# A chunked RWKV-7 recurrence with a gated feed-forward on one Trainium2 core: small TensorE tiles, back substitution on VectorE and a hand-written PE order

## Chip, cores and metric

The kernel runs on one core of a Trainium2 chip. The metric is the device time of one execution in microseconds (us). The kernel before took 1751.07 us, the median of three runs between 1740.38 and 1788.12.

## What is computed

Inputs are r, k, v, w, a, b of shape (4, 8, 768, 40) (batch, heads, steps, head width) and two weight matrices. For each of the 32 (batch, head) pairs a 40x40 state goes through 768 steps; the outputs are the rows of a 3072x320 matrix, and a feed-forward block follows:

```python
for t in range(S):
    y[:, :, t] = np.einsum('bhd,bhde->bhe', rt, state)
    Sa = np.einsum('bhde,bhe->bhd', state, at)
    state_decay = state * wt[:, :, None, :] - np.einsum('bhd,bhe->bhde', Sa, bt)
    state = state_decay + np.einsum('bhd,bhe->bhde', vt, kt)
...
h = x @ w_in          # 320 -> 2048
g = h * np.cos(h)
return (g @ w_out).astype(np.float32)   # 2048 -> 320
```

All arithmetic is float32. The two weight matrices arrive as float64 and are put together as float32 on the chip.

## The kernel before

The 768 steps are cut into 24 chunks of 32. Four batches times 32 steps fill the 128 partitions; the eight heads lie in the free dimension, and in transposed operands as four pairs of heads of 64 rows each (40 used). Names and lines are those of the listing below.

`prep(c)` (L208) makes what does not depend on the state. It transposes w, a, k, b, v, r (`turned`, L199), runs the product of decays with a scan (L217), divides (L219), and forms the products `gram` (L237 to 260). The inverse of a triangular 32x32 matrix per (batch, head), I + N, comes from five doubling steps (L262 to 289): VectorE transposes 32x32 blocks (L265) into a block-diagonal 128x128 tile `pbd`, PE multiplies with it (`power`), ScalarE and VectorE copy and add. `ttbd` holds the inverse, also block-diagonal.

`chain(c, ...)` (L302) carries the state over the chunk: `x0ps` (right-hand side), `snps` (times the inverse), `upd` (new state, L327 to 346), `sTps` and `mps` (the same solution transposed, times r), `yps` (outputs), `strn` (the new state transposed, through a multiplication with the identity), and four transposes `xps` that bring the outputs into `xT` for the feed-forward.

`first` (L402) and `second` (L423) are the feed-forward. `first` multiplies 256 tokens (two chunks) with w_in (`ph`, and a 64-row rest `w_in_tail`, in two row halves), and forms h*cos(h) with three VectorE and two ScalarE passes; `second` multiplies with w_out (`po`).

A matmul is recorded at the helper's line, L84; groups are told apart by their tiles. PSUM holds two buffers for `prep`, two for `chain`, three for `ph`, one for `po`. The order on every engine is made by a scheduler from the program's order: chunk c's `chain`, loads of chunk c+2 on SP's queue, `prep(c+1)`, then a part of the feed-forward of the two chunks before (`later`). The weights are read on ScalarE's DMA queue after `prep(0)`, in 28 pieces, each going through four VectorE, four GpSimd and one ScalarE instruction (`rounded`, L139).

Of the kernel before, what the change touches and what calls it, by code (L numbers as in the profile page):

```python
# [10 lines left out]
I32 = mybir.dt.int32  # L11
# [9 lines left out]
def kernel(  # L21
# [63 lines left out]


    nat = {n: kept(f"nat_{n}", [P, H, DP], 2, 1.0 if n == "w" else 0.0) for n in "wkabvr"}
# [3 lines left out]
    def load(c):  # L91
        for n in "wkabvr":
            for i in range(B):
                nc.sync.dma_start(
                    nat[n][c % 2][blk[i], :, :D],
                    src[n][i, :, c * C : (c + 1) * C, :].rearrange("h t d -> t h d"),
                )

    load(0)
    kn_b = kept("kn", [P, H, DP], 2, 0.0)  # L100
    bn_b = kept("bn", [P, H, DP], 2, 0.0)
    w0 = kept("w0", [P, NQ * B, C], 1, 0.0)[0]
    w1 = kept("w1", [P, NQ * B, C], 1, 0.0)[0]
    wx = kept("wx", [P, NQ * B, C], 1, 1.0)[0]
    pbd = kept("pbd", [P, 2, NQ, P], 1, 0.0)[0]
    ttbd_b = kept("ttbd", [P, 2, NQ, P], 2, 0.0)
    x0 = kept("x0", [P, 2, NQ, DP], 1, 0.0)[0]
    vbd = kept("vbd", [P, B, H, D], 1, 0.0)[0]
    snbd = kept("snbd", [P, B, 2, NQ, D], 1, 0.0)[0]
    st_b = kept("st", [P, NQ, B, DP], 2, 0.0)  # L110
# [4 lines left out]
    su = kept("su", [P, P], 1, 1.0)[0]  # L115

    nc.gpsimd.affine_select(
        su, su, pattern=[[1, P]], compare_op=ALU.is_gt, fill=0.0, base=0, channel_multiplier=-1
    )
    for s, base in ((1, 0), (-1, C - 1)):  # L120
        nc.gpsimd.affine_select(
            su, su, pattern=[[-C * s, B], [0, C]], compare_op=ALU.is_ge, fill=0.0, base=base,
            channel_multiplier=s,
        )
    su_c = kept("su_c", [P, C])[0]
    ident_c = kept("ident_c", [P, C])[0]
    for i in range(B):
        nc.gpsimd.tensor_copy(su_c[blk[i], :], su[blk[i], blk[i]])
        nc.gpsimd.tensor_copy(ident_c[blk[i], :], ident[blk[i], blk[i]])
    half_pi = kept("half_pi", [P, 1], 1, math.pi / 2)[0]  # L130
    su_q = su.unsqueeze(1).to_broadcast([P, NQ, P])
# [7 lines left out]
    def rounded(dst, src, by):  # L139


        n, cols = dst.shape[0], dst.shape[-1]
        words = sb2.tile([P, 512, 2], I32, tag="words", name="words")[:n, :cols]
# [347 lines left out]
```

## Time and profile before

| what | value |
|---|---|
| median of three runs | 1751.07 us |
| the profiled execution: its time | 1756.64 us |
| its span, first to last instruction | 1754.9 us |
| mean granted TensorE clock, of full speed (2.4 GHz) | 0.791 |
| instructions | 33475 |
| moved over HBM | 34.08 MB read, 3.93 MB written |

The profile comes from one execution. PE is TensorE's matmul part, PEld its weight loads, DVE VectorE, ACT ScalarE, POOL GpSimd, SP the queue of the sync engine, which issues DMAs. Busy time is the union of an engine's instructions; a matmul's own duration holds the depth of the pipeline, so that the pace of a run of matmuls is read from where the next group starts, not from the mean duration. The granted clock is the share of 2.4 GHz that TensorE was given; it has two levels, 0.5 and 1.

### The profile page before, as it was taken

Reading aid. Unit: us, or ns where it says so; the run is one execution under the profiler, and the core shown is the slowest. Engines: PE = TensorE matmul, PEld = TensorE weight load, DVE = VectorE, ACT = ScalarE, POOL = GpSimd, SP = SyncE. Lnnn points to the kernel's source line nnn. Section 1 sums busy time; section 2 is a strip of 40 time slices with the busy share of each in tenths; the row PEclk is TensorE's granted clock in tenths of the full one; section 3 lists DMA queues with packets and bytes.
Section 4 is the critical chain, followed back from the end, with each engine's and each line's share of the span. In section 5 each row is a group of like instructions: output and inputs, shape, how many; then the busy total and the mean of one; then the engine's idle time right before and its main releaser. Section 6 shows DMA issues by size and latency. Waiting matters only on the chain.

```text
span 1754.9 us, 33475 instructions
## 1 busy us (share of the span) xinstructions
PE 1664.4 (95%) x14464; PEld 1394.4 (79%) x14464; DVE 858.3 (49%) x1575; ACT 364.6 (21%) x796; POOL 154.5 (9%) x269
## 2 busy tenths in 40 slices
PE   4686999999999999999999999999999999999998
PEld 3676887887878888788788788788787888888876
DVE  8767453444454355355445444445436437436423
ACT  1122222131121122122212213113113112113112
POOL 3556000000000000000000000000000000000000
PEclk8555888778667778987878888878878889779779
DMA  4333111001100111111111100110010011000000
GB/s 84 93 88 76 17 20 19 14 12 19 24 12 12 20 16 20 20 16 20 20 16 18 20 16 15 20 20 13 16 28 12 12 23 21 13 13 1 1 9 8
DMA packets 165523, 40.20 MB, mean 23 GB/s; under 512 B 158720, under 2 KB 161792, under 8 KB 165376
## 3 DMA queue, kind: packets, MB, share of 16 engines
q1 hardware_dynamic: 161280, 27.57, 9.9%
q10 hardware_dynamic: 4096, 10.49, 2.0%
q8 instruction: 115, 1.88, 0.5%
q14 instruction: 32, 0.26, 0.0%
HBM read 34.08 MB, written 3.93 MB: 22 GB/s over the span
## 4 chain that ended last, share of the span: by engine, by line
PE 85%; DVE 9%; ACT 2%; issue 1%; POOL 1%; DMA 1%; SPq 0%; ACTq 0%; DVEq 0%; POOLq 0%
PE ph L84 16%; PE power L84 15%; PE po L84 14%; PE yps L84 9%; PE gram L84 6%; PE strn L84 6%; PE turned L204 5%; PE x0ps L84 4%; PE snps L84 3%; DVE pbd L265 2%; PE upd L84 2%; PE mps L84 2%; DVE rw L219 2%; ACT snbd L322 1%; PE xps L396 1%
## 5 line engine op out<-in xcount | busy, mean ns | idle before, releaser
L84 PEld LDWEIGHTS power<-pc,pbd 128*128 128x128 f32 x1920 | 282.2, 232 | 67.8 <-issue 49.4
L84 PE MATMUL power<-pc,pbd 128*128 128x64 f32 (+1 forms) x1920 | 291.5, 314 | 32.2 <-DVE pbd L265 28.1
L84 PE MATMUL ph<-xT,w_in_sb 128*128 128x256 f32 x768 | 246.6, 462 | 1.7 <-DVE gT L421 1.2
L84 PE MATMUL po<-w_out_sb,gT 128*128 128x320 f32 x768 | 247.4, 476 | 0.5 <-ACT ot L430 0.5
L265 DVE STREAM_TRANSPOSE pbd<-pc 32x256 f32<-32x256 f32 x480 | 208.3, 434 | 80.7 <-ACT pc L279 71.8
L84 PEld LDWEIGHTS po<-w_out_sb,gT 128*128 128x128 f32 x768 | 155.2, 210 | 61.6 <-issue 16.8
L84 PEld LDWEIGHTS ph<-xT,w_in_sb 128*128 128x128 f32 x768 | 164.6, 232 | 35.5 <-issue 11.0
L279 ACT COPY pc<-power 128x256 f32<-128x256 f32 x96 | 35.7, 372 | 518.3 <-PE power L84 512.3
L84 PE MATMUL ph<-xT,w_in_tail 64*128 64x256 f32 x384 | 112.8, 447 | 0.0
L283 DVE TENSOR_TENSOR pc<-power,pc 128x256 f32<-128x256 f32 x72 | 30.6, 425 | 158.1 <-ACT pc L279 157.9
L84 PE MATMUL yps<-bn,mbd 128*128 128x40 f32 x384 | 103.3, 364 | 0.0
L84 PE MATMUL yps<-kn,rvbd 128*128 128x40 f32 x384 | 100.9, 357 | 2.2 <-DVE mbd L360 2.2
L84 PE MATMUL strn<-ident,st 64*64 64x40 f32 x1472 | 98.2, 307 | 0.0
L84 PEld LDWEIGHTS strn<-ident,st 64*64 64x64 f32 x1472 | 94.7, 217 | 2.3 <-DVE frac L151 0.2
L217 DVE TENSOR_TENSOR_SCAN wp<-w,w 128x512 f32<-128x512 f32 x24 | 30.0, 1251 | 131.9 <-ACT w L215 131.9
L220 POOL COPY wx<-wp 128x496 f32<-128x496 f32 x24 | 14.3, 597 | 868.4 <-DVE wp L217 823.4
L84 PEld LDWEIGHTS yps<-kn,rvbd 128*128 128x128 f32 x384 | 84.2, 271 | 6.4 <-DVE mbd L360 3.1
L84 PEld LDWEIGHTS yps<-bn,mbd 128*128 128x128 f32 x384 | 86.8, 278 | 0.0
L389 ACT COPY s_nat<-strn 128x320 f32<-128x320 f32 x46 | 19.6, 425 | 313.3 <-PE strn L84 313.3
L84 PEld LDWEIGHTS ph<-xT,w_in_tail 64*128 64x128 f32 x384 | 59.9, 207 | 30.2 <-issue 25.0
L376 DVE TENSOR_TENSOR x<-yps,wxn 128x160 f32<-128x160 f32 x48 | 15.6, 325 | 139.5 <-PE yps L84 139.5
L219 DVE RECIPROCAL rw<-wp 128x512 f32<-128x512 f32 x24 | 80.3, 3347 | 0.4
(116 smaller groups left out, 2179.8 us busy)
## 6 DMA issues: line engine op xcount, KB each, us to landing
words<-in_moe_w_out_dram ACTq DMA_DIRECT2D x16, 320.0 KB, 3.0
words<-in_moe_w_in_dram ACTq DMA_DIRECT2D x8, 512.0 KB, 3.9
nat_w<-in_w_dram SPq DMA_DIRECT2D x96, 40.0 KB, 2.1
nat_k<-in_k_dram SPq DMA_DIRECT2D x96, 40.0 KB, 2.2
nat_a<-in_a_dram SPq DMA_DIRECT2D x96, 40.0 KB, 2.1
nat_b<-in_b_dram SPq DMA_DIRECT2D x96, 40.0 KB, 2.3
nat_v<-in_v_dram SPq DMA_DIRECT2D x96, 40.0 KB, 2.1
nat_r<-in_r_dram SPq DMA_DIRECT2D x96, 40.0 KB, 2.1
```

Of the source, the lines that this page charges most:

```text
L84: nc.tensor.matmul(o, lhsT=lhsT, rhs=rhs, start=start, stop=stop, skip_group_check=True)
L204: nc.tensor.transpose(ps[:, q, :], x[:, q, :], ident)
L217: nc.vector.tensor_tensor_scan(flat(wp), flat(w0), flat(w1), 0.0, ALU.mult, ALU.add)
L219: nc.vector.reciprocal(seq(rw), wp)
L220: nc.gpsimd.tensor_copy(wx[:, :, 1:], wp[:, :, : C - 1])
L265: nc.vector.transpose(pbd[blk[i], :, :, blk[i]].rearrange("p e q t -> p (e q) t"), heads(pc)[blk[i], :, 0, :],)
L279: nc.scalar.copy(heads(new)[:, :, 0, :], ps[:, :, 0, :])
L283: nc.vector.tensor_tensor(heads(new)[:, :, 1, :], ps[:, :, 1, :], heads(pc)[:, :, 1, :], ALU.add)
L322: nc.scalar.copy(snbd[blk[i], i], ps[blk[i]])
L376: nc.vector.tensor_tensor(by_parity(x)[:, e], ps, by_parity(g["wxn"])[:, e], ALU.mult)
L389: nc.scalar.copy(new_s[:, q0 : q0 + 2], ps)
L396: nc.tensor.transpose(ps[: min(P, DM - d0), i, :], xf[:, d0 : min(d0 + P, DM)], ident)
```

## The change

**Small tiles.** The block-diagonal 128x128 operands go. Matrices of one (batch, head) pair are multiplied in tiles of their own: 32 or 64 rows (where the operands lie) and 32 or 64 columns (where the output lies), in an order in which neighbours lie in other tiles. `nps` (N), `gram`, `x0ps`, `sps` (inverse times right-hand side), `dps` (state update and outputs) and `qps` are such groups.

**Transposed outputs from the update.** In `ch_x`, `ch_s` and `ch_z` the moving operand has 72 columns: 40 of the state's side and 32 of the output's side. So `dps` holds both the update of the state and the outputs, already transposed. `ch_t` transposes the state (8 PE transposes), `ch_q` multiplies it with r. The outputs go to a DRAM tile `xd` and come back as `xT`. `snps`, `sTps`, `mps`, `yps`, `strn` and `xps` go.

**Inverse.** N of four chunks is written to DRAM (`nd`) and read back with one (chunk, batch, head) per partition (`u`); VectorE does 31 steps of back substitution, two instructions each, and the result goes through DRAM (`rd`) back to the layout of the products (`rt`). The doubling steps and VectorE's transposes go.

**Order.** PE's instructions stand in the order of the program: per chunk the segments `ch_t`, `ch_q`, `ch_x`, `ch_s`, `ch_z`, after each a share of the preparation of later chunks (`p2_*` for the next, `p1_*` for the next four), then pieces of the feed-forward as they fall due, from chunk 4 on. The other engines are still ordered by the scheduler.

**Buffers and loads.** PSUM: two tiles of two banks for preparation and chain (`at`), two for `ph`, two for `po`. w, a and b are loaded in two halves per batch and chunk, k too, v twice. Weight pieces: one GpSimd pass and ScalarE's last pass become one ScalarE pass in the middle. In the feed-forward, the first of VectorE's three passes over `ph` is done by ScalarE and the second takes over an addition.

```diff
-    ps_pre = ctx.enter_context(tc.tile_pool(name="ps_pre", bufs=2, space=bass.MemoryType.PSUM))
-    ps_ch = ctx.enter_context(tc.tile_pool(name="ps_ch", bufs=2, space=bass.MemoryType.PSUM))
-    ps_h = ctx.enter_context(tc.tile_pool(name="ps_h", bufs=3, space=bass.MemoryType.PSUM))
-    ps_o = ctx.enter_context(tc.tile_pool(name="ps_o", bufs=1, space=bass.MemoryType.PSUM))
+    ps_a = ctx.enter_context(tc.tile_pool(name="ps_a", bufs=2, space=bass.MemoryType.PSUM))
+    ps_h = ctx.enter_context(tc.tile_pool(name="ps_h", bufs=2, space=bass.MemoryType.PSUM))
+    ps_o = ctx.enter_context(tc.tile_pool(name="ps_o", bufs=2, space=bass.MemoryType.PSUM))
...
+    def p1_n(c):
+        ps = at("nps")
+        for i in range(2):
+            for j in range(4):
+                for bb in range(B):
+                    for e in range(2):
+                        mm(
+                            ps[blk[bb ^ e], e, (4 * i + j) * C : (4 * i + j + 1) * C],
+                            G["bT", c + i][half[e], j, blk[bb]], G["aT", c + i][half[e], j, blk[bb]],
+                            i == 0 and j == 0,
+                        )
...
+    def inv_step(j):
+        u, x = (G[n].rearrange("p (s t) -> p s t", s=C) for n in ("u", "inv"))
+        tmp = sb1.tile([P, 16 * 17], F32, tag="inv_tmp", name="inv_tmp")
+        tmp = tmp[:, : j * (C - j)].rearrange("p (s t) -> p s t", s=j)
+        nc.vector.tensor_tensor(
+            tmp, u[:, :j, j : j + 1].to_broadcast([P, j, C - j]),
+            x[:, j : j + 1, j:].to_broadcast([P, j, C - j]), ALU.mult,
+        )
+        nc.vector.tensor_tensor(x[:, :j, j:], x[:, :j, j:], tmp, ALU.subtract)
...
+    def ch_t(c):
+        ps = at("sT")
+        G["s"] = sb1.tile([P, 2 * B, P], F32, tag="s", name="s")
+        for i in range(2 * B):
+            nc.tensor.transpose(
+                ps[:, i // 4, (i % 4) * P : (i % 4 + 1) * P], qz[:, i // 2, i % 2, C : C + P], ident
+            )
+        for i in range(2):
+            nc.scalar.copy(G["s"][:, 4 * i : 4 * i + 4].rearrange("p i e -> p (i e)"), ps[:, i])
...
+    def ch_z(c):
+        ps = [at("dps") for _ in range(2)]
+        sm = G["sm"]
+        for s, n in ((0, kn_b[c % 2]), (1, bn_b[c % 7])):
+            for j in range(4):
+                for bb in range(B):
+                    for pa in range(2):
+                        o = C - C * (j % 2)
+                        mm(
+                            ps[bb // 2][full[pa], bb % 2, j * N72 : (j + 1) * N72], n[blk[bb], j, pa, :],
+                            sm[blk[bb], pa, j, :] if s else vvm[c % 2][blk[bb], 4 * pa + j, o : o + N72],
+                            s == 0 and j == 0,
+                        )
...
+            n = sb3.tile([P, 4 * P], F32, tag="turns", name="turns")
+            nc.scalar.activation(n, u, ACTF.Identity, bias=rnd, scale=1.0)
+            nc.vector.scalar_tensor_tensor(n, n, -ROUND, u, ALU.add, ALU.subtract)
             nc.scalar.activation(n, n, ACTF.Abs)
             nc.scalar.activation(n, n, ACTF.Sin, bias=half_pi, scale=-2.0 * math.pi)
...
+        START, done, n_seg = 4, 0, 0
+        for c in range(NCH):
+            q0 = c - c % 4 + 4
+            side = []
+            if c + 1 < NCH:
+                side += [lambda: p2_v(c + 1), lambda: p2_k(c + 1), lambda: p2_g(c + 1)]
+            if q0 < NCH and c % 4 < 2:
+                side += p1(q0 + 2 * (c % 4))
+            main = ([lambda: ch_t(c), lambda: ch_q(c)] if c else []) + [
+                lambda: ch_x(c), lambda: ch_s(c), lambda: ch_z(c),
+            ]
+            n = len(main)
+            for i, seg in enumerate(main):
+                seg()
+                for s in side[len(side) * i // n : len(side) * (i + 1) // n]:
+                    s()
+                due = (c + (i + 1) / n - START) / (NCH - START) * len(pieces) * 0.97
+                while done < due and 2 * pieces[done][0] + 2 <= c:
+                    pieces[done][1]()
+                    done += 1
```

How the order moves, at three places. First PE, in the preparation of a chunk before (`gram` and `power` are the products and the doubling steps, `ph` the feed-forward):

```order
L84 MATMUL gram<-rT,vT 128x128 x8
L84 MATMUL ph<-xT,w_in_sb 128x256
L84 MATMUL power<-pc,pbd_138 128x32 x8
L84 MATMUL ph<-xT,w_in_sb 128x256 x3
L84 MATMUL ph<-xT,w_in_tail 128x256 x2
L84 MATMUL power<-pc,pbd_138 128x64 x8
L84 MATMUL ph<-xT,w_in_tail 128x256 x2
L84 MATMUL ph<-xT,w_in_sb 128x256 x4
L84 MATMUL power<-pc,pbd_138 128x64 x8
L84 MATMUL ph<-xT,w_in_tail 128x256 x2
L84 MATMUL x0ps<-nat_v_92,abd 128x40 x4
```

and PE now, in a chunk without `p1` (`dps` takes both buffers of preparation and chain, `gram` is the next chunk's, `po` and `ph` are pieces of the feed-forward):

```order
L97 MATMUL ph<-xT,w_in_sb 128x256 x8
L97 MATMUL ph<-xT,w_in_tail 128x256 x4
L97 MATMUL x0ps<-vvm_105,ag 32x72 x32
L97 MATMUL x0ps<-qz_107,aT 32x72 x32
L97 MATMUL po<-w_out_sb,gT 128x320 x8
L97 MATMUL sps<-x_6671,rt 32x72 x32
L226 MATMUL kT<-ident_157,kn_192 128x128 x4
L97 MATMUL ph<-xT,w_in_sb 128x256 x8
L97 MATMUL ph<-xT,w_in_tail 128x256 x4
L97 MATMUL dps<-vvm_105,kn_190 64x72 x32
L97 MATMUL dps<-sm,bn_182 64x72 x32
L97 MATMUL gram<-aT,kT 32x32 x32
```

The doubling steps with feed-forward in their waits are gone; feed-forward pieces of one kind stand between the segments of the chain, and `gram` follows `dps` at once.

Second VectorE at the start. Before, the masks of chunk 0 (`pc`, `abd`, `rvbd`) and the transposes stand before most of the weight pieces (`mant`, `expo`):

```order
L244 TENSOR_TENSOR pc<-gram,su_c_164 128x4x32 x2
L248 TENSOR_TENSOR pc<-ident_c_165,pc 128x8x32
L265 STREAM_TRANSPOSE pbd_138<-pc 32x8x32
L260 TENSOR_TENSOR abd<-gram,su_159 128x512
L265 STREAM_TRANSPOSE pbd_138<-pc 32x8x32
L260 TENSOR_TENSOR abd<-gram,su_159 128x512
L265 STREAM_TRANSPOSE pbd_138<-pc 32x8x32
L260 TENSOR_TENSOR rvbd<-gram,su_159 128x512
L265 STREAM_TRANSPOSE pbd_138<-pc 32x8x32
```

Now the inverse (`inv_tmp`, `inv`) of the first four chunks begins behind some twelve weight pieces:

```order
L179 SCALAR_TENSOR_TENSOR mant<-words,mant 128x320
L188 SCALAR_TENSOR_TENSOR expo<-words,expo 128x320
L178 TENSOR_SCALAR mant<-words 128x320
L183 TENSOR_SCALAR expo<-words 128x320
L319 TENSOR_TENSOR inv_tmp<-u,inv 128x31
L179 SCALAR_TENSOR_TENSOR mant<-words,mant 128x320
L323 TENSOR_TENSOR inv<-inv,inv_tmp 128x31
L319 TENSOR_TENSOR inv_tmp<-u,inv 128x60
L188 SCALAR_TENSOR_TENSOR expo<-words,expo 128x320
L323 TENSOR_TENSOR inv<-inv,inv_tmp 128x30x2
```

and the first mask of the chain, `sm`, stands behind all but one:

```order
L183 TENSOR_SCALAR expo<-words 128x320
L179 SCALAR_TENSOR_TENSOR mant<-words,mant 128x320
L188 SCALAR_TENSOR_TENSOR expo<-words,expo 128x320
L178 TENSOR_SCALAR mant<-words 128x320
L183 TENSOR_SCALAR expo<-words 128x320
L179 SCALAR_TENSOR_TENSOR mant<-words,mant 128x320
L188 SCALAR_TENSOR_TENSOR expo<-words,expo 128x320
L453 TENSOR_TENSOR sm<-sps,su_162 128x2x64
L371 TENSOR_TENSOR ag<-gram,su_162 128x256
L453 TENSOR_TENSOR sm<-sps,su_162 128x2x64
```

So chunk 0's chain now waits on VectorE's queue for the weights.

Third SP's queue in the steady stretch. Before, it had only loads and the stores of the output:

```order
L433 DMA out_dram<-ot 32x320 x8
L94 DMA nat_v_94<-in_v_dram 32x8x40 x4
L94 DMA nat_w_76<-in_w_dram 32x8x40 x4
L94 DMA nat_a_84<-in_a_dram 32x8x40 x4
L94 DMA nat_r_96<-in_r_dram 32x8x40 x2
L94 DMA nat_k_80<-in_k_dram 32x8x40 x4
```

and now, in the second chunk of four (`nd`, `u`, `xd`, `xT` are the ways through DRAM):

```order
L127 DMA nat_w_81<-in_w_dram 32x4x40 x2
L299 DMA nd<-nt 128x512
L505 DMA xT<-xd 128x2x128
L507 DMA xT<-xd 64x128 x2
L127 DMA nat_w_81<-in_w_dram 32x4x40
L303 DMA u<-nd 8x32x32 x8
L127 DMA nat_w_81<-in_w_dram 32x4x40 x5
L127 DMA nat_a_85<-in_a_dram 32x4x40 x8
L127 DMA nat_b_89<-in_b_dram 32x4x40 x8
L127 DMA nat_w_83<-in_w_dram 32x4x40 x8
L127 DMA nat_a_87<-in_a_dram 32x4x40 x8
L127 DMA nat_b_91<-in_b_dram 32x4x40 x8
```

The ways through DRAM stand among the loads, and the 48 loads of w, a and b of two chunks stand almost in one row.

## Rows read from the trace of the kernel before

**Rows 1.** Page, part 1: engine, busy us (share of the span), instructions.

```profile
PE 1664.4 (95%) x14464; PEld 1394.4 (79%) x14464; DVE 858.3 (49%) x1575; ACT 364.6 (21%) x796; POOL 154.5 (9%) x269
```

**Rows 2.** Page, part 4: the chain that ended last, shares by engine.

```profile
PE 85%; DVE 9%; ACT 2%; issue 1%; POOL 1%; DMA 1%; SPq 0%; ACTq 0%; DVEq 0%; POOLq 0%
```

**Rows 3.** Stages: us; busy us of PE, PEld, DVE, ACT, POOL; clock, DMA, GB/s.

```profile
0.00:220.00 220.00, 158.23 (x1259) 141.35 (x1259) 149.32 (x280) 40.98 (x91) 95.50 (x147) 0.67 0.32 71
220.00:1700.00 1480.00, 1458.08 (x12960) 1217.64 (x12959) 693.03 (x1269) 311.44 (x684) 59.00 (x122) 0.81 0.10 16
1700.00:1755.00 55.00, 48.09 (x250) 35.39 (x249) 15.91 (x26) 12.22 (x21) 0.00 (x0) 0.89 0.03 7
```

**Rows 4.** Groups of PE, shapes apart: count | busy us, mean ns | idle before.

```profile
L84 PE MATMUL power<-pc,pbd 128*128 128x64 f32 x1152 | 164.1, 304 | 25.4 <-DVE pbd L265 21.3 <-ACT w_out_sb L164 3.3
L84 PE MATMUL yps<-bn,mbd 128*128 128x40 f32 x384 | 103.3, 364 | 0.0
```

**Rows 5.** Timeline of PE in a steady stretch: start us, us, records.

```profile
1015.54 0.76 PE L84 MATMUL yps<-s_nat,rT 40*32 40x40 f32 x32
...
1049.68 0.49 PE L84 MATMUL x0ps<-st,aT 40*32 40x40 f32 x32
1050.10 1.08 PE L84 MATMUL x0ps<-nat_v,abd 128*128 128x40 f32 x8
...
1069.33 0.66 PE L204 MATMUL turned<-ident,nat_a 128*128 128x128 f32 x4
1069.82 0.60 PE L204 MATMUL turned<-ident,nat_k 128*128 128x128 f32 x4
...
1085.85 4.24 PE L84 MATMUL strn<-ident,st 64*64 64x40 f32 x64
```

**Rows 6.** Timeline of PE in the last stretch, feed-forward work alone.

```profile
1713.49 1.13 PE L84 MATMUL ph<-xT,w_in_tail 64*128 64x256 f32 x8
...
1716.47 1.13 PE L84 MATMUL ph<-xT,w_in_tail 64*128 64x256 f32 x4
...
1721.78 3.72 PE L84 MATMUL ph<-xT,w_in_sb 128*128 128x256 f32 x16
...
1741.85 8.88 PE L84 MATMUL po<-w_out_sb,gT 128*128 128x320 f32 x32 [0.52 <-ACT ot L430]
```

**Rows 7.** Short stretches by busy time and granted clock, columns as in rows 3.

```profile
1015.40:1016.30 0.90, 0.90 (x34) 0.73 (x35) 0.00 (x0) 0.00 (x0) 0.00 (x0) 0.50 0.00 0
1049.60:1050.20 0.60, 0.60 (x35) 0.50 (x34) 0.59 (x2) 0.00 (x0) 0.00 (x0) 1.00 0.00 0
1086.00:1090.00 4.00, 4.00 (x64) 3.94 (x64) 0.31 (x1) 0.43 (x1) 0.00 (x0) 0.50 0.02 4
1722.00:1740.00 18.00, 18.00 (x76) 13.06 (x76) 10.09 (x16) 6.72 (x11) 0.00 (x0) 1.00 0.00 0
1113.00:1122.00 9.00, 8.93 (x50) 6.71 (x49) 4.84 (x11) 2.00 (x4) 0.00 (x0) 1.00 0.00 0
```

**Rows 8.** Timeline of the start: SP's loads, the weight pieces on POOL.

```profile
3.54 3.77 SPq L94 DMA_DIRECT2D nat_k<-in_k_dram  x4
...
7.43 1.88 SPq L94 DMA_DIRECT2D nat_a<-in_a_dram  x4
...
97.84 0.72 POOL L163 TENSOR_TENSOR frac<-frac,expo 128x256 f32<-128x256 f32 x1 [0.54 <-DVE expo L160]
...
169.48 0.86 POOL L163 TENSOR_TENSOR frac<-frac,expo 128x320 f32<-128x320 f32 x1
```

**Rows 9.** Groups of DVE, shapes apart: two sizes of one operation.

```profile
L421 DVE TENSOR_TENSOR gT<-ph,turns 128x512 f32<-128x512 f32 x96 | 65.5, 682 | 6.9 <-ACT turns L419 5.0
...
L244 DVE TENSOR_TENSOR pc<-gram,su_c 128x128 f32<-128x128 f32 x48 | 13.9, 291 | 29.4 <-PE gram L84 29.4
```

**Rows 10.** One tensor, nat_w: its loads on SP (ns), and time to landing.

```profile
L94 SPq DMA_DIRECT2D nat_w<-in_w_dram x96: 311/442/1188, 1.5 to 1484.2; - x96
...
DMA to landing us min/median/max: 1.8/2.1/5.5
```

More of the change, by code (lines that the diff above doesn't have):

```diff
@@ L99 @@
[L99 to L110, printed above, removed]
+    padding = lambda t: t[:, :, :, D:]
@@ L113, with load_vv @@
+    def load_vv(c):
+        for i in range(B):
+            nc.sync.dma_start(
+                vvm[c % 2][blk[i], :, C : C + D],
+                v[i, :, c * C : (c + 1) * C, :].rearrange("h t d -> t h d"),
+            )
+    load(0, "wab")
+    load(1, "wab")
     ident = kept("ident", [P, P])[0]
     make_identity(nc, ident)
[L115 to L119, printed above, removed]
@@ L379, in chain @@
-        if new_st is not None:
-            for q0 in range(0, NQ, 2):
-                ps = ps_ch.tile([P, 2, B, D], F32, tag="ch", name="strn")
-                for q in (q0, q0 + 1):
-                    for e in range(2):
-                        for i in range(B):
-                            mm(
-                                ps[full[e], q - q0, i, :], new_st[full[e], q, i, :],
-                                ident[full[e], half[e]], q == q0 and i == 0,
-                            )
-                nc.scalar.copy(new_s[:, q0 : q0 + 2], ps)
@@ L460, with second @@
-    for work in later:
-        work()
+            nc.vector.tensor_tensor(
+                G["gT", j][:, 2 * e : 2 * e + 2].rearrange("p f t -> p (f t)"), u, n, ALU.mult
+            )
+    def second(g, j, i):
+        if j == 0:
+            G["po", i] = ps_o.tile([P, DM], F32, tag="o", name="po")
+        po = G["po", i]
+        for f in range(4):
+            mm(
+                po, G["gT", j][:, f, i * P : (i + 1) * P], w_out_sb[:, 4 * j + f, :],
+                j == 0 and f == 0, j == NF // 4 - 1 and f == 3,
+            )
+        if j == NF // 4 - 1:
+            ot = sb2.tile([P, DM], F32, tag="ot", name="ot")
+            nc.scalar.copy(ot, po)
+            for bb in range(B):
+                t0 = bb * S + (2 * g + i) * C
+                nc.sync.dma_start(out[t0 : t0 + C, :], ot[blk[bb], :])
@@ new lines, in inverse @@
+    def inverse(c, part):
+        steps = list(range(C - 1, 0, -1))
+        lo, hi = ((0, 12), (12, 31))[part]
+        if part == 0:
+            inv_start(c)
+        for j in steps[lo:hi]:
+            inv_step(j)
+        if part == 1:
+            inv_end(c)
+    with tc.manual_schedule(engines={mybir.EngineType.PE}):
+        for seg in p1(0):
+            seg()
+        load(0, "kvr")
+        load_vv(0)
+        load_vv(1)
+        load(2, "wab")
+        load(3, "wab")
+        for seg in p1(2):
+            seg()
+        load(4, "wab")
+        load(5, "wab")
+        inverse(0, 0)
+        inverse(0, 1)
+        p2_v(0)
+        p2_k(0)
+        p2_g(0)
+        load_weights()
+        START, done, n_seg = 4, 0, 0
[8 more added lines that the diff above has]
+                lambda: ch_x(c), lambda: ch_s(c), lambda: ch_z(c),
+            ]
+            n = len(main)
+            for i, seg in enumerate(main):
+                seg()
+                for s in side[len(side) * i // n : len(side) * (i + 1) // n]:
[4 more added lines that the diff above has]
+                    done += 1
+            if c + 2 < NCH:
+                load_vv(c + 2)
+            if q0 < NCH and c % 4 >= 2:
+                if c % 4 == 2 and q0 + 4 < NCH:
+                    load(q0 + 4, "wab")
+                    load(q0 + 5, "wab")
+                inverse(q0, c % 4 - 2)
+            if q0 < NCH and c % 4 == 0:
+                load(q0 + 2, "wab")
+                load(q0 + 3, "wab")
+        for _, work in pieces[done:]:
+            work()
```

545 lines of the change are left out of this document (301 added, 244 removed).

## Prediction

> **What bounds the kernel now.** I read the page's busy shares first: TensorE works in 95% of the span, VectorE in 49%, ScalarE in 21% [rows 1]. The chain that ended last says the same, 85% of it is PE [rows 2]. So this kernel is bound by TensorE's work, and the table by stage says where: from 220 to 1700 us PE is busy for 1458.1 of 1480 us, at a mean granted clock of 0.81; the first 220 us hold the start (158.2 us of PE work), the last 55 us one group of feed-forward work [rows 3]. A chunk of the recurrence (24 of them) takes about 1480/22 = 67 us. Engines that are not PE hide behind it today; whether they still do is the question, because the change cuts PE's work.
>
> What is PE's work? Every fp32 matmul stands in the trace as two records, a transpose as one. The costliest groups belong to the recurrence's full-size tiles: the doubling steps `power` with 64 columns alone are 164.1 us, the 40-column `yps` products 103.3 us for one half of them [rows 4]. They pay for loading 128 columns of weights to move 32 to 64 columns. A small tile pays far less: 32 records of `x0ps<-st` (16 matmuls, output in one quarter of the partitions, the quarters taking turns) start at 1049.68 and the next group starts at 1050.10, 0.42 us, so 26 ns per matmul, against 1.08 us for the next 8 records (4 matmuls) with 128x128 tiles, 270 ns [rows 5]. That ratio is what the change lives on.
>
> **The change part by part.** The span of the profiled execution is 1754.9 us, its time 1756.6 us (1.7 us around it), the median of the three runs 1751.07; I sum against the profiled one.
>
> *Feed-forward work (kept).* Per group of two chunks: `ph` has 64 records at 3.72/16 = 0.2325 us, 14.9 us; its tails 32 records at 1.13/8 = 0.141, 4.5 us; `po` 64 records at 8.88/32 = 0.278, 17.8 us [rows 6]. Sum 37.2 us at the full clock (1.00 in this stretch [rows 7]), 446 us for 12 groups. The tails also show that two tiles on different row halves run side by side: 8 records that alternate between the halves take 1.13 us, 4 on one half take 1.13 us too [rows 6]. The change relies on this for its tiles of 32 rows.
>
> *Recurrence on PE.* `power`, `snps`, `sTps`, `mps`, `strn`, `xps` and the full-size `gram`, `x0ps`, `yps` go. In their place stand, per chunk: 36 transposes, and 288 small matmuls (nps 32, gram 64, qps 32, x0ps 64, sps 32, dps 64). Four transposes from 1069.33 to 1069.82 take 0.49 us, 0.122 each [rows 5]: 4.4 us. 288 x 0.026 = 7.5 us. Together 11.9 us per chunk at the full clock. No row of before has 32-row tiles, 64-column tiles with eight in turn, or 72 moving columns; bounds: 0.015 (eight instead of four in turn) and, from the same kind of tile at half the clock (`yps<-s_nat`, 0.76 us for 32 records, 24 ns each [rows 5, 7]), 0.048 per matmul. I take 0.026, the nearest row. 20 chunks (4 to 23) make 238 us; the last four have no preparation of later chunks (16 transposes, 32 small ones, 2.8 us each) and the last one no second part (3.1 us): 224 us.
>
> *Steady stretch, chunks 4 to 23.* The hand-written order lets 174 of the 192 feed-forward pieces run there (a piece of group g waits until chunk 2g+2, so group 11 comes after the loop): 446 x 174/192 = 404 us. With 224 that is 629 us at the full clock. The clock: 0.50 beside `yps<-s_nat` and while `strn` runs alone, 1.00 in the stretches of `ph` and `po`, and of `po` mixed with other work [rows 7]. As feed-forward pieces now stand every few us, I take 0.92; bounds 1.00 (629 us) and before's 0.79 (796). 629/0.92 = 684 us. To that come waits of PE. Four PSUM buffers for the preparation and chain become two double ones; after `dps`, which takes both, the next user waits for two additions and two outputs on VectorE (from the fit 0.16 us + 1.02 ns per element below, about 1.3 us); kT to gram and bT to nps wait for a ScalarE copy. I count 4.5 us in chunks with preparation, 1.5 in the others, 60 us; and 6 us each at chunks 20 and 22, where pieces were held back until the outputs of the chunk just ended have gone through DRAM. Together 72 us, bounds 30 and 120. The stretch: 756 us.
>
> *Start.* Here something is added. The matrix inverse of four chunks needs their decays: 96 loads of w, a and b, with 24 of k, v and r and 9 issues of the way through DRAM among them, 129 at 1.88/4 = 0.47 us on SP [rows 8], 61 us, an estimated 4 for landings and 10 from the last load to the mask: 75 us for the second pair of chunks. VectorE takes its instructions in order, and behind that pair's mask stand 26 of 28 weight pieces; the inverse's 62 instructions lie among them and the first `sm` of the chain behind all but one piece. Before, the last 16 pieces came at (169.48 - 97.84)/16 = 4.48 us each [rows 8], so chunk 0 goes on at 75 + 25 x 4.48 = 187, plus an estimated 8 to its end. The inverse itself: two VectorE operations show 291 ns at 128 columns and 682 at 512 [rows 9], so 0.16 us + 1.02 ns per element, and 62 instructions over 10,912 elements make 21 us, half in the waits of the weights; bounds 0 and 21, I add 5 on this path. Chunks 1 to 3 have no feed-forward work to lie beside and a cold clock: 36 transposes at twice 0.122, 8.8; 288 x 0.048, 13.8; some 3 us of waits: 26 us, 78 for three. Chunk 4 starts at 187 + 8 + 5 + 78 = 278; bounds 240 and 310. Before, PE had useful work there; this stretch gives back part of the gain.
>
> *End.* Wait for the last outputs through DRAM (two transfers of 2.1 us [rows 10] and their VectorE, GpSimd and issue times, 9 us), 18 pieces, 42 us, and 4 for the last output: 55 us, as long as before's last stretch.
>
> *Other engines.* VectorE loses 480 transposes and gains six inverses (127 us): some 20 us per chunk, under PE's 36. ScalarE takes over one of the three VectorE passes over `ph`, at about VectorE's 0.68 us: some 15 us per chunk, estimated from that row. Both cost nothing as long as PE's pieces cover them. SP is closer: its issues go from 672 to 1,483, 62 per chunk at 0.47 us, 29 us, plus about 4 us of waiting for DRAM tiles to land. That still hides under 36 us, with little to spare; if not, C below.
>
> Sum: 278 + 756 + 55 = 1089 us, with 1.7 around the span **1091 us**.
>
> **Rivals.**
> A, the forecast, 1091.
> B, the small tiles let the clock fall: mean 0.6 in the loop, 629/0.6 = 1048, 364 more, 1455. For it: 0.50 beside `strn` [rows 7]. Against: mixed stretches of `po` stand at 1.00.
> C, SP sets the pace. The loads of k at the start took 3.77/4 = 0.94 us each [rows 8]; then 62 x 0.94 + 4 = 62 us per chunk, 20 x 62 + 278 + 55 = 1573, with the 1.7 us 1575. Against: the median of the w loads is 0.44 us [rows 10], and 0.94 fell beside the weights' transfer.
> D, the round trip of the state (transpose, q, x, s, z and a copy between each) is not covered, since PE takes pieces in order: 20 x (26 + 404/0.92/20 = 22) = 960, with start and end 1295.
> E, on the other side: tiles do not run side by side over row groups, and each small matmul costs what `strn` costs, 4.24/32 = 132 ns at half the clock [rows 5, 7], place: all chain and preparation products. (132 - 26) x 288 = 30.5 us per chunk, 20 x 30.5 + 3 x 24 = 682, 1773; the 160 of 288 that move 72 columns instead of 40 raise it, in proportion, by 160 x 0.106 = 17 us a chunk, to some 2100; I put 1900, slower. It decides from (1757 - 1091)/23/288 = 0.1 us more per matmul, 127 ns. Against: the alternating tails [rows 6].
> F, small matmuls do not start closer than 24 ns a record (`yps<-s_nat` at half the clock) at any clock: 576 x 0.024 = 13.8 instead of 7.5 us per chunk, 126 more, 1217. Against: 0.42 us for 32 records, 13 ns each, at clock 1.00 [rows 5, 7].
> The Trainium skill, "TensorE: Matmul & The Clock Gate" (section "Wait — 56ns, not 53.3ns?"), says that matmuls never start closer together than about 25 ns however few columns they move, which would speak against this change; by it 14.4 us a chunk and some 1230 us. The 13 ns just shown disagree, and the measurement decides, so F gets a small chance.
>
> **How the numbers follow.** A 0.66, D 0.09, B 0.07, C 0.07, F 0.07, E 0.04. The sum of the lower bounds is 240 + 629 + 30 + 50 = 949, of the upper ones 310 + 796 + 120 + 60 = 1286; the small tiles' own bounds (63 less, 127 more) would widen that if all ends met, which I leave out. The range 960 to 1300 takes in A, F and D and leaves out B, C and E, 0.18. All but E are far over 2% faster (2% is about what a measurement of this kernel tells from no change): faster 0.95, same 0.01, slower 0.04.
>
> **What would show it.** Right: a span near 1090 with chunk 4 near 280 us, PE at about 9 tenths after it, a granted clock over 0.9 there, 32 small matmuls (64 records) in about 0.8 us, and the doubling's groups gone. Wrong: records of small tiles at 60 ns or more (E), 24 ns at clock 1.00 (F), a clock near 0.6 (B), PE idle before loads whose issue stands late on SP (C), PE idle at each chain step for a copy (D), or a start over 310 us.

## The result and the profile after

The changed kernel takes 1181.04 us (median; 1179.24 to 1182.34) against 1757.92 for the kernel before, a ratio of 0.674 (95% interval 0.668 to 0.680). The forecast was 1091, so the result lies inside its range and 90 us over the forecast itself. The page of the kernel after, parts 1 and 2 (busy us; 40 slices of 29.5 us, in tenths), and the first line of part 4, against [rows 1, 2]:

```profile
PE 838.5 (71%) x16472; PEld 644.0 (55%) x16472; DVE 507.9 (43%) x1109; ACT 344.0 (29%) x651; POOL 200.8 (17%) x342
...
PE   2140025474688888888987896976977977979878
...
PEclk9975555755689988989888998888987986979879
...
PE 41%; SPq 22%; DVE 14%; DMA 7%; issue 7%; ACT 6%; POOL 3%; POOLq 0%; DVEq 0%; ACTq 0%
```

PE's busy time is halved (1664 to 838 us) with more records than before (14,464 to 16,472), and PE is no longer the one bound: 85% of the last chain was PE, now 41%, and SP's queue holds 22%. By stage (columns as in [rows 3]; the borders are the ends of chunks 3 and 23, the last `dps` record of each in the timeline):

```profile
0.00:288.10 288.10, 95.38 (x2644) 77.06 (x2644) 156.94 (x342) 45.77 (x93) 90.69 (x152) 0.65 0.39 80
288.10:1125.70 837.60, 699.92 (x13653) 535.40 (x13652) 339.46 (x749) 281.36 (x530) 108.82 (x189) 0.86 0.27 49
1125.70:1180.10 54.40, 43.16 (x176) 31.54 (x176) 11.47 (x20) 16.92 (x28) 1.26 (x1) 0.88 0.07 19
```

Start 288 (forecast 278), end 54.4 (55), loop 837.6 (756): of the 90 us that were missed, 82 are in the loop. There PE works 700 us (forecast 684) and stands idle 138 (forecast 72). Where it stands, in PE's timeline of chunk 12 (630.7 to 685.9 us), and in the waits of PE over the loop (us in total, times, longest):

```profile
632.60 0.82 PE L97 MATMUL gram<-aT,kT 40*32 40x32 f32 x60 [1.86 <-DVE yt L487]
...
647.60 1.08 PE L226 MATMUL vT<-ident,nat_v 128*128 128x128 f32 x4 [5.92 <-DMA nat_v<-in_v_dram]
...
659.76 0.73 PE L97 MATMUL gram<-aT,kT 40*32 40x32 f32 x62 [1.14 <-ACT kT L351]
...
660.98 2.42 PE L97 MATMUL po<-w_out_sb,gT 128*128 128x320 f32 x8
...
665.06 0.88 PE L97 MATMUL x0ps<-vvm,ag 32*32 32x72 f32 x64
665.87 0.89 PE L97 MATMUL x0ps<-qz,aT 40*32 40x72 f32 x64
666.69 1.09 PE L226 MATMUL wT<-ident,nat_w 128*128 128x128 f32 x8
...
678.41 1.09 PE L256 MATMUL wn<-ident,wp 128*128 128x128 f32 x4 [3.65 <-DVE sm L453]
```

```profile
PE gram L97 <- DVE yt L487: 32.3, 12, 6.5
PE bT L226 <- DVE yt L487: 20.3, 8, 4.2
PE vT L226 <- DMA nat_v<-in_v_dram: 16.8, 3, 6.7
PE gram L97 <- ACT kT L351: 13.8, 8, 4.1
PE ph L97 <- DMA xT<-xd: 11.3, 4, 5.0
PE wn L256 <- DVE sm L453: 11.1, 8, 3.7
```

The small matmuls are as cheap as hoped: 64 records of `x0ps` (32 matmuls of 72 columns) from 665.06 to 665.87, 25 ns a matmul; `gram`, 128 records from 659.76 to 660.98, 19 ns; `dps` 24 and `qps` 33, all at a granted clock of 1.00; over a chunk 6.9 us for 288, where the forecast had 7.5. What grew is the idle time. VectorE ends 69 us of it, ScalarE 25 and a DMA 37 (sums over the whole list). `gram` and `bT` wait for `yt` because `dps` holds both of the double PSUM buffers until VectorE has read them, and `vT` waits for loads that SP issued late. SP's timeline ahead of that wait, and SP's own waits in the loop:

```profile
612.20 3.77 SPq L127 DMA_DIRECT2D nat_w<-in_w_dram  x8
...
636.33 3.75 SPq L127 DMA_DIRECT2D nat_b<-in_b_dram  x8
640.12 3.75 SPq L127 DMA_DIRECT2D nat_k<-in_k_dram  x8
643.92 1.91 SPq L122 DMA_DIRECT2D nat_v<-in_v_dram  x4
```

```profile
SPq L498 <- POOL wx L248: 74.1, 8, 24.2
SPq L133 <- PE dps L97: 56.0, 16, 14.5
SPq L498 <- POOL yt L492: 50.4, 5, 34.5
SPq L556 <- ACT ot L553: 35.4, 8, 10.5
```

The loads of v stand behind 48 loads of w, a and b, 27.9 us in a row, and those behind SP's writes of `xd` and the outputs, for which it had to wait. From these rows came two theories: P, the turn-around of the PSUM buffers, and S, SP's queue.

### The profile page after: what moved, and what is told of

Read it like the earlier page. It is cut to its first block, busy times and chain, and to the rows that moved or that the text cites. A ratio compares the mean times of both kernels' runs of the same rounds, so it can differ in the third digit from the quotient of the medians.

```text
span 1180.1 us, 37667 instructions
## 1 busy us (share of the span) xinstructions
PE 838.5 (71%) x16472; PEld 644.0 (55%) x16472; DVE 507.9 (43%) x1109; ACT 344.0 (29%) x651; POOL 200.8 (17%) x342
## 4 chain that ended last, share of the span: by engine, by line
PE 41%; SPq 22%; DVE 14%; DMA 7%; issue 7%; ACT 6%; POOL 3%; POOLq 0%; DVEq 0%; ACTq 0%
SPq L127 16%; PE ph L97 15%; PE po L97 13%; DVE inv_tmp L319 2%; DVE inv L323 2%; DVE rw L261 2%; PE x0ps L97 2%; PE dps L97 2%; ACT turns L536 1%; SPq L122 1%; PE bT L226 1%; PE nps L97 1%; PE gram L97 1%; ACT turns L535 1%; DVE wp L245 1%
## 5 line engine op out<-in xcount | busy, mean ns | idle before, releaser
L97 PE MATMUL ph<-xT,w_in_sb 128*128 128x256 f32 x768 | 202.9, 419 | 18.2 <-DMA xT<-xd 18.1
L534 DVE SCALAR_TENSOR_TENSOR turns<-turns,ph 128x512 f32<-128x512 f32 x96 | 61.6, 682 | 276.5 <-ACT turns L533 276.5
L533 ACT ACTIVATE turns<-ph,rnd 128x512 f32<-128x512 f32 x96 | 60.7, 684 | 203.1 <-PE ph L97 203.1
L537 DVE TENSOR_TENSOR gT<-ph,turns 128x512 f32<-128x512 f32 x96 | 65.9, 690 | 63.8 <-ACT turns L536 63.5
L319 DVE TENSOR_TENSOR inv_tmp<-u,inv 128x31 f32<-128x31 f32 (+15 forms) x186 | 70.8, 381 | 5.3
L323 DVE TENSOR_TENSOR inv<-inv,inv_tmp 128x31 f32<-128x31 f32 (+15 forms) x186 | 68.1, 366 | 5.0
L536 ACT ACTIVATE turns<-turns,half_pi 128x512 f32<-128x512 f32 x96 | 68.9, 722 | 2.3
L535 ACT ACTIVATE turns<-turns 128x512 f32<-128x512 f32 x96 | 59.4, 624 | 10.3 <-DVE turns L534 10.3
L97 PE MATMUL ph<-xT,w_in_tail 64*128 64x256 f32 x384 | 54.8, 404 | 0.0
L261 DVE RECIPROCAL rw<-wn 128x320 f32<-128x320 f32 x24 | 51.6, 2149 | 4.5 <-PE wn L226 4.2
```

The source lines that it names most:

```text
L97: nc.tensor.matmul(o, lhsT=lhsT, rhs=rhs, start=start, stop=stop, skip_group_check=True)
L261: nc.vector.reciprocal(rw, unpad(ps[:, 0].rearrange("p (j a d) -> p j a d", a=2, j=4)))
L319: nc.vector.tensor_tensor(tmp, u[:, :j, j : j + 1].to_broadcast([P, j, C - j]), x[:, j : j + 1, j:].to_broadcast([P, j, C - j]), ALU.mult,)
L323: nc.vector.tensor_tensor(x[:, :j, j:], x[:, :j, j:], tmp, ALU.subtract)
L533: nc.scalar.activation(n, u, ACTF.Identity, bias=rnd, scale=1.0)
L534: nc.vector.scalar_tensor_tensor(n, n, -ROUND, u, ALU.add, ALU.subtract)
```

## The experiments

All are edits of the changed kernel. "Start" is the time to the end of chunk 3, "idle" the loop less PE's busy time in it, "by DMA" the part of the idle time that a transfer ends. Most have two runs, up to 0.9% apart, and differences in time of less than 1% are not read; the other columns come from one profile each.

| run | time us | start | loop | PE busy | idle | by DMA | clock |
|---|---|---|---|---|---|---|---|
| changed kernel | 1181.0 | 288 | 838 | 700 | 138 | 37 | 0.86 |
| k, v, r first | 1188.2 | 283 | 849 | 707 | 142 | 41 | 0.85 |
| pieces first | 1195.8 | 286 | 858 | 717 | 141 | 23 | 0.85 |
| both | 1180.0 | 282 | 838 | 706 | 132 | 14 | 0.87 |
| scheduler's order | 1183.1 | 300 | 824 | 715 | 109 | 2 | 0.86 |
| even order | 1184.0 | 291 | 836 | 687 | 149 | 64 | 0.88 |
| weights early | 1172.6 | 274 | 841 | 702 | 139 | 37 | 0.86 |
| no back substitution | 1168.8 | 271 | 845 | 699 | 146 | 51 | 0.86 |
| same tile in a row | 1493.2 | 341 | 1098 | 1059 | 39 | 6 | 0.80 |
| queues | 1164.0 | 274 | 830 | 695 | 135 | 21 | 0.86 |
| even and queues | 1152.4 | 276 | 813 | 677 | 136 | 31 | 0.89 |
| that, split weights | 1189.4 | 304 | 828 | 674 | 154 | 33 | 0.86 |
| that, xT on GpSimd | 1119.3 | 259 | 804 | 679 | 125 | 27 | 0.89 |

**k, v, r first.** The loads move from the preparation step to the end of the chunk before, ahead of w, a and b.

```diff
-        load(c + 1, "kvr") if c + 1 < NCH else None
...
+            if c + 3 < NCH:
+                load(c + 3, "kvr")
             if c + 2 < NCH:
                 load_vv(c + 2)
```

> The loads of k, v and r are taken out of the preparation step and issued one chunk earlier, ahead of the 48 loads of w, a and b in a row on SP. Theory S (in the loop of the changed kernel SP delivers late: PE's idle time before the transposes of v and r, 16.8 + 4.4 us, is a queue on SP): these two waits go to under 5 us, the loop from 838 to about 815 us, the time from 1181 to about 1155-1165. Theory P (PE's idle time is that of the double PSUM buffers after dps, and whatever SP does is covered): the waits for nat_v and nat_r go, but the time stays within 10 us of 1181, since the wait returns at the next user of a buffer. Rival (the same number of issues comes out late somewhere else, at xT or at w and a): the sum of PE's waits that a DMA ends stays near 37 us.

The waits for v and r went, those for w and a came (13.9 and 9.4 us): a row of issues in another order is as late in another place.

**Pieces first, and both.** PE's order alone: the feed-forward pieces that are due come ahead of the preparation's steps; then together with the edit above.

```diff
                 seg()
+                due = ...
+                while done < due and 2 * pieces[done][0] + 2 <= c:
+                    ...
                 for s in side[len(side) * i // n : len(side) * (i + 1) // n]:
                     s()
```

> Only PE's written order changes: after each step of the chain the feed-forward pieces that are due come first, then the preparation steps of later chunks, so that 2 to 10 us of feed-forward work stand between dps, which takes both PSUM buffers, and the next user of one. Theory P (buffers): the waits of gram and bT for yt, 32.3 + 20.3 us, go to under 10 us, the loop from 838 to 790-800 us, the time to 1130-1145; the granted clock rises a little from 0.86. Theory S (SP): the time stays within 10 us of 1181, as the loads are no earlier. Rival D (the round trip of the state is the bound): the chain's steps stand no further apart than before, so the idle time moves to sT, qps, x0ps and sps and the time stays.

> Both edits of the two runs before together. If buffers (P) and SP's queue (S) each hold PE up by themselves, the gains add: 1105-1125 us. If one wait lies under the other, the time is that of the better one alone. If both fall, 1181.

The waits for `yt` shrank to a few us, but now `dps` waited 39.8 us in front, for the `aT` that VectorE makes from the buffer it needs. The wait had only changed sides. Together the two give nothing either.

**Scheduler's order.** One part of the change undone.

```diff
-    with tc.manual_schedule(engines={mybir.EngineType.PE}):
+    if True:
```

> One part of the change undone: the PE order written by hand (the program order inside the manual schedule) is left to the scheduler again, with small tiles, back substitution and everything else kept. If the hand order is what lets the small tiles' gain through: 1230-1350 us, with PE idle before chain steps and a clock under 0.86. If the gain is that of the small tiles alone and any order with feed-forward pieces among them does: 1160-1200 us.

1183.1: the order written by hand is worth nothing that can be measured here. The scheduler starts the feed-forward work at 248 us and not at 304, and the start is 12 us longer, the loop 99 records shorter. In the loop the idle time falls by 28 us, yet PE's busy time rises by 15 at the same clock; why it rises was not looked into.

**Even order.** The steps of a chunk in one list, and a piece wherever one is due after each.

```diff
+                seq = [(st, 0), (vv, 1), (qq, 0), (kk, 1), (xx, 0), (gg, 1), (pw, 0), (ss, 1),
+                       (a0, 1), (a1, 1), (zz, 1), (pb, 1), (pn, 1)]
+            elif c + 1 < NCH:
+                seq = [(st, 1), (vv, 1), (qq, 1), (kk, 1), (xx, 1), (gg, 1), (ss, 2), (zz, 2)]
...
+            for seg, weight in seq:
+                seg()
+                i += weight
+                due = (c + i / n - START) / (NCH - START) * len(pieces) * 0.97
```

> After the first four runs: moving the wait for a PSUM buffer from behind dps to ahead of it gave nothing (the waits for yt went, 40 us of dps waiting for VectorE's aT came). Here the written PE order puts one feed-forward piece between nearly every two users of the double buffers, ahead of dps and behind it too; nothing else changes. Theory P2 (PE's idle time in the loop is the double buffers' turn-around wherever two users stand together): all waits for yt, aT, kT, bT and sm fall to under 40 us in sum, the loop from 838 to 770-790 us, the time to 1115-1135, the granted clock in the loop over 0.88. Theory L (the loop is bound by another chain: mask of nps, way through DRAM, back substitution, way back, sps, once in four chunks, with VectorE in between): the waits change their places again and the time stays within 12 us of 1181.

PE's waits in its loop:

```profile
PE ph L97 <- DMA xT<-xd: 25.1, 4, 12.9
PE vT L226 <- DMA nat_v<-in_v_dram: 22.9, 3, 8.0
PE gram L97 <- issue: 15.7, 8, 2.9
PE dps L97 <- DVE aT L263: 13.2, 9, 2.5
PE wT L226 <- DMA nat_w<-in_w_dram: 13.0, 2, 6.9
```

The engines' share of the idle time fell from 94 to 55 us, the DMAs' rose from 37 to 64. P2 was right about the buffers and wrong about the time: waits for transfers came in their place.

**Weights early** and **no back substitution.** `load_weights()` ahead of `p1(0)`; and, in another kernel, the two VectorE instructions of each of the 31 steps left out, so that the inverse is not computed.

```diff
+    load_weights()
     with tc.manual_schedule(engines={mybir.EngineType.PE}):
...
-        load_weights()
```

```diff
-        for j in steps[lo:hi]:
-            inv_step(j)
+        del steps[lo:hi]
```

> Only the place of the 28 weight pieces in the program changes: ahead of the preparation, not behind it, so VectorE, idle for 50 of the first 75 us, takes them first. Theory V (the start is held by VectorE's order: 26 pieces between the second mask and the back substitution): the pieces are done by about 100 us, the 62 instructions of the back substitution run alone in some 23 us instead of 45, chunk 0 ends at about 140 instead of 194 us, and the time falls by 40-55 us to 1125-1140. Theory C (beside the weights' transfer SP's loads take 2 to 3 us each instead of 0.47): the loads of the second pair come by so much later, the mask moves from 75 to 130 us or more, and the time is within 10 us of 1181 or above it.

> The back substitution's 62 VectorE instructions per four chunks are left out (the way to and from DRAM stays), so the inverse is not computed. Theory L (the back substitution lies on the path of every fourth chunk): start 25 to 45 us shorter, and each of the five later ones 5 to 10 us, 1085-1130 us. Theory P2 (in the loop it is covered by feed-forward work): only the start gets shorter, 1135-1155 us; loop within 10 us of 838. My prediction took 5 us on the path at the start and none in the loop: 1170-1180 us.

Early weights bring chunk 0's end from 194 to 180 us, not to 140: the masks of the two pairs, which SP had sent off at 34 and 76 us, wait behind the weight pieces and leave at 114 and 122. Without the steps chunk 0 ends only 4 us earlier, because there another wait comes to light: in PE's order the transposes of the next chunk's v stand ahead of chunk 0's `sps`, and SP issues these loads late (SP's and PE's timeline of that run):

```profile
159.69 4.03 SPq L122 DMA_DIRECT2D nat_v<-in_v_dram  x4
...
166.13 1.09 PE L226 MATMUL vT<-ident,nat_v 128*128 128x128 f32 x4 [83.11 <-DMA nat_v<-in_v_dram]
```

The start gains 17 us, 11 of them in chunk 3, where the changed kernel has this row among PE's waits (194 to 288 us):

```profile
PE sps L97 <- DVE x L430: 11.1, 1, 11.1
```

There VectorE has the next four chunks' back substitution ahead of the copy of `x`. In the loop it costs nothing (845 against 838 us).

**Same tile in a row.** The loops of all small products are turned inside out, here for `x0ps`:

```diff
-        for j in range(4):
-            m, e = j // 2, j % 2
-            for bb in range(B):
-                for pa in range(2):
+        for bb in range(B):
+            for pa in range(2):
+                for j in range(4):
+                    m, e = j // 2, j % 2
```

> The loops around the small matmuls are turned inside out: the four or eight with the same partitions of weights and of output now follow each other, where before the tiles took turns; number, sizes and PSUM places are the same. If small tiles are cheap only because neighbours lie in different tiles: 25 ns or more per record (7.5 to 12 before at the full clock), 576 records x 15 ns x 23 chunks = 200 us more, 1300-1400 us. If the price is that of the few columns and rows alone: 8 to 12 ns a record still, and 1175-1190 us.

PE's timeline, the same groups as above:

```profile
810.25 2.64 PE L97 MATMUL x0ps<-vvm,ag 32*32 32x72 f32 x64
812.82 2.65 PE L97 MATMUL x0ps<-qz,aT 40*32 40x72 f32 x64
815.39 1.09 PE L226 MATMUL wT<-ident,nat_w 128*128 128x128 f32 x8
```

2.57 us for what took 0.81, both at a granted clock of 1.00: 80 ns a matmul (40 a record) instead of 25, and 1493 us, over the expected range. The 312 us that this costs are more than half of the change's gain of 577: so much hangs on tiles that take turns. The rest (no doubling steps, transposed outputs) was not taken apart.

**Queues.** ScalarE issues the output stores, GpSimd the writes of `xd`, and `vvm` gets its values by a GpSimd copy of `nat_v`.

```diff
-                nc.sync.dma_start(out[t0 : t0 + C, :], ot[blk[bb], :])
+                nc.scalar.dma_start(out[t0 : t0 + C, :], ot[blk[bb], :])
...
-            nc.sync.dma_start(
+            nc.gpsimd.dma_start(
                 xd[4 * D * e : 4 * D * (e + 1)].rearrange("(j d) t -> d j t", j=4),
...
+        nc.gpsimd.tensor_copy(
+            vvm[c % 2][:, :, C : C + D], nat["v"][c % 2].rearrange("t i e d -> t (i e) d")[:, :, :D]
+        )
```

> PE's order stays as in the changed kernel. Taken off SP is what makes it wait in the loop: the outputs' stores are issued by ScalarE, the writes of xd by GpSimd, and the values in vvm are copied on chip by GpSimd from nat_v, without a second load (12 of 62 issues a chunk less, and 259 us of SP's waits behind yt, dps and ot gone). Theory PS (PE's loads are late because SP stands in order behind those waits, and the buffers' turn-around costs as much again): waits of PE that a DMA ends fall from 37 to under 12 us, but the waits for yt, kT and sm stay, 1145-1160 us. Theory S alone: 1100-1130 us. Theory L (another chain): 1170-1185 us.

> The even PE order of an earlier run (buffer waits down to some 45 us, waits for loads and xT up to 64 us, time unchanged) together with the queues of the run before this one. Theory PS (the two kinds of waits lie under each other, so that taking away either one shows nothing): now the loop falls from 838 to 740-770 us, the time to 1085-1115. Theory L: 1165-1185 us, with PE's waits moved to steps of the chain.

Alone the queues take 8 us from the loop and 14 from the start, 1164 in all, between the ranges of PS and L. Even order alone took 1 us from the loop, both together take 24. That looks like waits that lie under each other, but the loop of both together says otherwise:

```profile
276.10:1089.40 813.30, 677.47 (x13525) 517.10 (x13524) 338.98 (x752) 278.10 (x529) 142.40 (x248) 0.89 0.25 47
```

PE is idle for 136 us, as good as in the changed kernel (138). Of the 24 us, 22 are less busy time, 677 us for 700, at a granted clock of 0.89 instead of 0.86. Theory PS had asked for a loop of 740 to 770 us, and it fell. The waits only moved once more: 82 us of the idle time end with VectorE, ScalarE or GpSimd (55 in the even order alone), 31 with a DMA (64). And SP went on waiting, for the same data one step later (SP's waits of "queues", in the loop):

```profile
SPq L508 <- DMA xd<-yt: 180.4, 15, 54.2
```

**Split weights; xT on GpSimd.** The first run issues column block 0 ahead of the preparation, block 1 between its pairs, blocks 2 and 3 behind the first inverse, with START 3. The second has all weights early, START 4, and the reads into `xT` on GpSimd:

```diff
-        nc.sync.dma_start(xT[:, :2, toks], xd[: 2 * P].rearrange("(i p) t -> p i t", p=P))
+        nc.gpsimd.dma_start(xT[:, :2, toks], xd[: 2 * P].rearrange("(i p) t -> p i t", p=P))
         for e in range(2):
-            nc.sync.dma_start(xT[full[e], 2, toks], xd[2 * P :])
+            nc.gpsimd.dma_start(xT[full[e], 2, toks], xd[2 * P :])
```

> Even order and queues as before, and the start as well: the weight pieces of two of eight... of the first two of four column blocks are issued ahead of and between the two preparation steps, the rest stays behind the first inverse, and feed-forward pieces are due from chunk 3 on, not 4. Theory V (at the start VectorE and the queue hold chunk 0): chunk 0 ends at 140-160 instead of 194 us, first ph at 230-250 instead of 304, the time 40-55 us under that of the run before this one. If the weights' transfer slows SP's loads in the same measure: within 15 us of it.

> Even order and queues as in the run that took 1152 us; there SP still stood for 195.6 us of the loop waiting for the writes of xd to land, since the reads into xT were left on it, with loads behind. Here GpSimd issues those reads too, and the 28 weight pieces stand ahead of the preparation as in an earlier run (which alone gave 9 us at the start). Theory PS: PE's waits in the loop that a DMA ends go from 38 us to under 20, the loop from 813 to about 790 us, and the start gives its 9 us: 1115-1130 us, faster than every kernel before. If what is left of PE's idle time is the chain and its evictions and not SP: the loop stays at 805-820 and only the start's 9 us come, 1140-1150 us.

Split weights fell: chunk 0 ends at 192 us again, and pieces in chunk 3 make it 46 us long instead of 27. The last run, 1119.26 us (four runs, 1115.30 to 1123.44), ratio to the kernel before 0.641 (0.637 to 0.645), beats both kernels (the changed one has 0.674). Its stages and the first of PE's waits in its loop:

```profile
0.00:258.90 258.90, 92.47 (x2772) 75.60 (x2772) 164.09 (x341) 46.68 (x94) 110.51 (x172) 0.87 0.42 88
258.90:1063.20 804.30, 679.13 (x13525) 518.74 (x13524) 339.02 (x750) 278.22 (x529) 180.07 (x308) 0.89 0.25 47
1063.20:1119.60 56.40, 42.47 (x176) 31.03 (x176) 11.48 (x20) 16.92 (x28) 4.45 (x6) 0.86 0.07 19
```

```profile
PE ph L97 <- DMA xT<-xd: 25.5, 4, 7.1
PE gram L97 <- issue: 18.2, 9, 2.7
PE dps L97 <- DVE aT L263: 14.0, 10, 2.5
PE bT L226 <- ACT bT L274: 12.5, 8, 5.5
```

In the loop no load of w, a, b or k and only 1.7 us of v and r hold PE up any more, but with `xT` a DMA still ends 27 us of its waits (under 20 expected). The time was in the expected range for a partly other reason. Against the run before (even and queues), the start is 17 us shorter (9 expected) and the loop 9 (23 expected). Against the changed kernel, 29 of the 62 us are at the start. Of the 33 in the loop, only 12 are less idle time; 21 are less busy time for nearly the same records, with the granted clock at 0.89 and not 0.86.

## Why the prediction was right, and where it was off

The mechanism held. PE was the bound, the full-size products paid for weights, and small tiles in turns cost what [rows 5] said: 25 ns for `x0ps` and 19 for `gram`, against 26 taken. Rivals E (132 ns) and F (24 ns a record; measured 9.5 to 17 at clock 1.00) fall. The Trainium skill, "TensorE: Matmul & The Clock Gate" (section "Wait — 56ns, not 53.3ns?"), says that two matmuls never start less than about 25 ns apart. For `gram` that does not hold, counted by matmul (19 ns) or by record (9.5). Rival E's worry was half true: without turns a matmul of 72 columns costs 80 ns, under E's 127, so the change would still have been faster (1493).

The end was 54.4 us for 55. The start, 288 for 278, is right only in sum. The second mask came at 75.5 us (75), and chunk 0 ended at 194 (200 forecast: 187, 8 to its end and 5 for the inverse). What held it is what the forecast named: the chain that ended last runs from 77 to 180 us through the weight pieces, their transfer and the inverse among them, and the first `sm` starts on VectorE right behind a piece:

```profile
179.67 0.28 DVE L453 TENSOR_TENSOR sm<-sps,su 128x128 f32<-128x128 f32 x1
```

Two errors of size partly cancel: weight pieces of 320 columns took 2.9 us instead of 4.48, and the steps of the inverse spread over 45 us (21 taken). SP's lateness lies beneath. Beside the weights' transfer it took up to 3 us an issue instead of 0.47, rows of its timeline:

```profile
78.65 16.84 SPq L303 DMA_DIRECT2D u<-nd  x8
95.53 20.98 SPq L127 DMA_DIRECT2D nat_b<-in_b_dram  x7
...
164.78 15.48 SPq L332 DMA_DIRECT2D rt<-rd  x16
```

That is rival C's mechanism, in the one stretch where [rows 8] had shown it, and it sets the end of chunk 0 when the inverse's steps are left out. Chunks 1 to 3 took 94 us (78), 11 of them behind the back substitution, whose price I had put at 5 on the path; the run without it says 17, all at the start.

The step that failed is "Together 72 us, bounds 30 and 120", the waits of PE in the loop: 138. I had counted 4.5 us in a chunk with preparation (`p1`) and 1.5 in the others; for the eight chunks that have it this makes 54 us, not the 60 that I wrote. PE's idle time chunk by chunk is 82 us in these eight, 10.3 each, 36 in the eight others up to 19, 4.5 each, and 19 in the last four (18).

Two parts of the term were too small. One is the turn-around of the double buffers: I had taken some 1.3 us behind `dps`, and `gram` and `bT` waited 2.7 and 2.5 us there on average; I had named the copies ahead of `gram` and `nps`, but not the second `wn`, which waits for `sm` (11.1 us). The other is SP, put at nothing: I had let it hide "with little to spare" by adding up its issues (29 us a chunk) and 4 us of landings, without its waits, some 260 us of 838, most of them behind `xd`, `dps` and the outputs. SP took its instructions in order in these traces, so that a store that waited held up the loads behind it, and 37 us of PE's idle time end with a DMA.

The clock term was 0.92 and came out at 0.86, and that PE's 700 us lie so near to 684 is partly luck. At 0.86 the forecast's 629 us of work would have taken 731, 47 more. But 700 us at 0.86 are an estimated 602 at the full clock, 27 less than 629, 12 of them from the small matmuls (6.9 us a chunk for 7.5). Two signs of being right did not come: PE at 9 tenths in the loop (84%) and a granted clock over 0.9. Yet this is not rival B, the small tiles by themselves, as these rows show: one of the changed kernel, behind the 1.86 us that PE stood idle before `gram`, and two chunks of the last run with all their small tiles.

```profile
632.60:634.00 1.40, 1.40 (x128) 1.40 (x128) 0.71 (x4) 0.00 (x0) 1.40 (x4) 0.50 0.30 43
...
347.70:386.10 38.40, 35.99 (x773) 27.30 (x774) 14.56 (x39) 15.54 (x29) 7.52 (x14) 1.00 0.37 65
386.10:419.50 33.40, 30.84 (x629) 23.12 (x629) 28.27 (x72) 14.48 (x27) 7.32 (x13) 1.00 0.28 62
```

What lowers the clock elsewhere was not taken apart; with the same tile in a row it is 0.80, though PE hardly stands idle.

The Trainium skill says in "TensorEngine Tiling (Array Packing)" (section "PSUM Bottleneck") that tiles speed up TensorE but not the reading of PSUM, which may then set the pace, and the trace agrees: 94 of the 138 us end with VectorE's or ScalarE's reading.

What stays open: in every run with tiles in turns the idle time lies between 109 and 154 us, whatever wait was taken away, and in none was it the 72 of the forecast. With slower PE work (same tile in a row) it is 39, so it is latency that PE's work no longer covers. Which chain of steps sets it was not settled. Not tried: a slower pace of the pieces, and buffers of one PSUM bank, so that `dps` leaves one free. In chunk 21 one piece stands and in chunk 23 none, since the next group's wait for their outputs. Chunk 23 shows the chain's round trip nearly bare: 17 us, 4 of them idle, where rival D took 26.

## What to carry to other kernels

When a change halves the work of the engine that bounds a kernel, forecast the rest from the queues in order: add up what each engine issues together with what it waits for, because a wait holds up everything behind it. Where several waits lie beneath each other, taking away one or two may only move them: here the idle time stayed within 109 to 154 us in twelve kernels. So read busy and idle time of that engine apart, and the idle time by what ends it, before a gain in time is put down to a theory: a higher granted clock can look like a wait that went. Small tiles are cheap when neighbours lie in different tiles, so write the tile index as the innermost loop.

## What was not expected of the hardware

- The same 64 records at the same granted clock (1.00) took 0.81 us with tiles in turns and 2.57 us with the same tile in a row.
- 8 loads of 20 KB take SP 3.75 us, 4 loads of 40 KB 1.91 us: 0.47 us an issue for both sizes, and up to 3 us while the weights' transfer runs.
- GpSimd issued two writes of `xd` in 1.34 us, 0.67 us each, where SP had taken 0.69 us for the two; GpSimd was busy for 142 of the loop's 830 us.
